# A seven-product down projection for the second group of the gated layer, with block 0's sum held in DRAM, and another written order of the opening

## The chip, the cores and the metric

The kernel runs on one core of a Trainium2 chip. The metric is the device time of one execution in microseconds (us), the median of three runs. The core's engines run side by side and each works through its own queue in the order in which the program writes it: TensorE (PE in the profile, with its weight loads as PEld), VectorE (DVE), ScalarE (ACT), GpSimd (POOL) and the queue that issues most transfers (SP).

## The reference

Three stages follow each other. The first is a retention layer over 2 batches of 8 heads, 768 positions and 64 features per head; its output is reshaped to 1536 tokens of 512 features. Then comes a gated layer of width 1536, then a leaky layer of width 2048:

```python
state = gamma * state + k_t (x) v_t;  y_t = scale * q_t . state      # per batch and head
xn = x / sqrt(mean(x * x) + 1e-6) * rms_g
x  = (silu(xn @ w_gate) * (xn @ w_val)) @ w_out                      # 512 -> 1536 -> 512
h  = x @ w_in
out = maximum(0.01 * h, h) @ w_out2                                  # 512 -> 2048 -> 512
```

All inputs and the output are float32.

## The kernel before

**Retention.** The 1536 positions are 12 chunks of 128, six for each batch. For a chunk `c` the program computes the scores (`sc`), masks them (`ds`), multiplies with the values (`he`), adds what the state of the chunks before gives (`yi`, with queries decayed by `qs`), and updates the state (`kd` decays the keys, `ou` is the outer product, `up` the update). `kd` runs on DVE for the chunks listed in `KD` and as eight small ACT operations for the others. The norm of two chunks at a time goes `sq`, `fa`, `sa` (squares and sums), `to` (total over features, PE), `me` (mean, DVE), `rs` (power -0.5, POOL), `sp` (spread over rows, PE), `xs` (scale), `hi` and `lo` (a rounded high part and the rest).

**Products with split operands.** A float32 operand is kept as a high and a low part, and a product of two operands is three matmuls: high by high, high by low, low by high. Tokens are in three blocks of 512 (`b` = 0, 1, 2). A full product of one 128-wide slice `f` of a layer for one block is 12 matmuls of 128x512.

**Weights.** The weights arrive as 64-bit raw words (512 KB for each slice, tile pool `raws` with 3 buffers, fetched in the queue of SP at L387). Each is converted by two ACT operations (`P`), five DVE operations (`1`, `2`, `3`, `4`, `L`) and one ACT operation (`H`). Converted weights live in 12 slots of the pool `units`, and in 2 more after the retention stage.

**Groups.** The gated layer has 12 slices in groups 0, 1 and 2 of four (kinds `g`, `v` and the down projection `o`); the leaky layer has 16 slices in groups 3 to 6 (kinds `i` and down projection `p`).

**Quads.** For two slices and the blocks 1 and 2 together, `quad` takes seven half products of 6 matmuls in place of eight (42 matmuls in place of 48); it needs two more weight operands made by sums (`sg4` and `sg5` from `g4` and `g5`), each sum key costing six DVE and two ACT operations. Block 0 takes full products (`whole`). The first two slices, `g0`, `g1`, `v0`, `v1`, are plain.

**Down projections.** `down` takes one slice and one block: the hidden block is split (`upper`, an ACT copy at L611, and `lower`, a DVE subtraction at L619) and goes into four PSUM banks in 12 matmuls. After the last slice of a group and block, `evac1` (gated layer) or `evac2` (leaky layer) adds the four banks into an SBUF sum. For the four groups of the leaky layer (the set `seven`, from `SEVEN = 4`) the blocks 1 and 2 of the down projection take the same seven-product scheme: `gather` collects the hidden tiles, `seventh` issues 6 matmuls for each of seven products of a slice pair, `follow` forms the next operand by a DVE subtraction (L704), and the results go from two banks at a time into the sums by DVE (L767). Block 0 of these groups takes plain `down` and is added into the output in DRAM by an accumulating transfer issued from POOL (L800).

**The order.** Everything up to the fourteenth product is written out by hand in `ORDER`: tokens of two letters and a chunk, conversion steps such as `v0:3`, and from `layers` on the products (`Mg01` is the first eight matmuls of slice g0 in block 1, `Ng01` its other four, `C` its evacuation, `Do00` a down projection, `T`, `Th`, `Tl` the sums for the quads). `LOADS` is the order of the first transfers (`q`, `k` a chunk's queries and keys or keys and values of 512 KB; `m` mask, `d` query decays, `s` state decays, `g` norm gains, `i` identity, `w` a raw weight); `load` then adds `q11` and `k11`. After the fourteenth product, `run` places conversions, sums and splits between the products by a small planner with costs (0.6 and 0.34 us for DVE operations, 2.72 us for a product).

Of the kernel before, what the change touches and what calls it, by code (L numbers as in the profile page):

```python
# [16 lines left out]
P = 128  # L17
# [10 lines left out]
HEAD = "dddd0"  # L28
# [34 lines left out]
def chain_kernel(ctx: ExitStack, tc: tile.TileContext, qk_t, kv, w1, w2, mask, qdec, kdec, sdec, rms_g, ident, out):  # L63
# [19 lines left out]
    ps_acc = ctx.enter_context(tc.tile_pool(name="ps_acc", bufs=1, space=bass.MemoryType.PSUM))  # L83
    attn_pools = ctx.enter_context(ExitStack())
# [5 lines left out]

    mask_sb = const.tile([P, 2, NPAIR, CH], F32, name="mask_sb")
# [299 lines left out]
    def open_unit():  # L391
# [12 lines left out]
        if src is None:  # L404
# [229 lines left out]
    def down(gi, f, b):  # L634
        kinds, fs = groups[gi]
        L = kinds[-1]
        key = (L, f, b)
        upper(key)
        lower(key)
        accumulate(L, gi, f, b, f == fs[0], f == fs[-1], L == "o" or b > 0)  # L640
        used(f"{L}{f}")
        if f == fs[-1]:
            banks = acc.pop("b")
            first = gi in (0, len(G1))
            by_copy = first or L == "p" and b == 0 and gi < len(groups) - 1
            later.append(("a" if by_copy else "v", 2.4, lambda: (evac1 if L == "o" else evac2)(gi, b, banks)))
        placed[0] = order.index(key) + 1

    def evac1(gi, b, banks):
        if gi == 0:  # L650
            acc[b] = xp.tile([P, 4, 512], F32, tag=f"acc{b}", name=f"x2acc{b}")
        last = gi == len(G1) - 1
        own = range(2, 4) if b == 2 else range(4)
        if last:
            x2h[b] = xp.tile([P, 4, 512], F32R, tag=f"xh{b}", name=f"x2h{b}")
            x2l[b] = xp.tile([P, 4, 512], F32R, tag=f"xl{b}", name=f"x2l{b}")
        for m in range(4):
            dst = acc[b][:, m, :]
            if gi == 0:
                nc.scalar.activation(out=dst, in_=banks[m], func=AF.Copy)  # L660
            else:
                nc.vector.tensor_tensor(out=dst, in0=banks[m], in1=dst, op=ALU.add)  # L662
        if last:
            def high(m):
                nc.scalar.activation(out=x2h[b][:, m, :], in_=acc[b][:, m, :], func=AF.Copy)

            def low(m):
                nc.vector.tensor_tensor(
                    out=x2l[b][:, m, :], in0=acc[b][:, m, :], in1=x2h[b][:, m, :].bitcast(F32), op=ALU.subtract
                )  # L670

            highs, lows = ([lambda m=m, do=do: do(m) for m in own] for do in (high, low))
            if b == 2:
                one, two = slice(0, 2), slice(2, 4)
                ops = sums_of(
                    acc, x2h, x2l, acc[1][:, one], acc[1][:, two], x2h[2][:, one], x2l[2][:, one], extra()[:, two]
                )
                first_of = [lambda i=i: [ops[n]() for n in (f"{i}", f"h{i}")] for i in range(4)]
                sums.extend(first_of[:2] + [ops["l1"]] + highs + [ops["l0"]] + lows)
                sums.extend([first_of[2], ops["l2"], first_of[3], ops["l3"]])  # L680
            else:
                sums.extend(highs + lows)
# [35 lines left out]

    def seventh(gi, n, f):
        fs = groups[gi][1]  # L720
        key = ("q", f, n)
# [8 lines left out]
        names = f"p{f}", f"p{f + 1}", f"sp{f}", f"sp{f + 1}"  # L730
# [153 lines left out]
    def place(n, key, own=None):  # L884
# [3 lines left out]
        if n == "i" and key[1] == 0:  # L888
            return extra()[:, key[0] % 4, :]
# [46 lines left out]
    def quad(n, f):  # L936
# [62 lines left out]
    def plan():  # L999
# [12 lines left out]
        for gi, (kinds, fs) in enumerate(groups):  # L1012
# [26 lines left out]
            if gi in seven:  # L1039
# [247 lines left out]
```

## Time and profile before

| what | us |
|---|---|
| median of three runs | 582.78 |
| lowest and highest | 582.76, 582.89 |
| the profiled execution | 583.3 |
| its span, first to last instruction | 581.3 |

The profile describes one execution. Its span is 2.0 us shorter than that execution's own time, and that execution is 0.52 us above the median. PE is busy for 98% of the span, DVE for 87%, ACT for 61%.

### The profile page before, as it was taken

Reading aid. Unit: us, or ns where it says so; the run is one execution under the profiler, and the core shown is the slowest. Engines: PE = TensorE matmul, PEld = TensorE weight load, DVE = VectorE, ACT = ScalarE, POOL = GpSimd, SP = SyncE. Lnnn points to the kernel's source line nnn. Section 1 sums busy time; section 2 is a strip of 40 time slices with the busy share of each in tenths; the row PEclk is TensorE's granted clock in tenths of the full one; section 3 lists DMA queues with packets and bytes.
Section 4 is the critical chain, followed back from the end, with each engine's and each line's share of the span. In section 5 each row is a group of like instructions: output and inputs, shape, how many; then the busy total and the mean of one; then the engine's idle time right before and its main releaser. Section 6 shows DMA issues by size and latency. Waiting matters only on the chain.

```text
span 581.3 us, 8448 instructions
## 1 busy us (share of the span) xinstructions
PE 571.3 (98%) x3107; PEld 471.1 (81%) x3107; DVE 505.8 (87%) x921; ACT 355.9 (61%) x652; POOL 26.6 (5%) x28
## 2 busy tenths in 40 slices
PE   7899999999999999999999999999999999999997
PEld 4788788888888888888888878888888888888885
DVE  4899999999578579697688999999999999997793
ACT  2689656776565464554564667877856885676330
POOL 2332100000000000000000000000000020002000
PEclk9999999999999999999999999999999999999999
DMA  8991240433222221221411111113411353111545
GB/s 327 408 392 59 73 144 1 145 110 115 67 73 73 72 74 31 78 72 38 144 37 36 38 36 37 57 53 108 173 39 43 109 142 78 36 37 19 127 85 133
DMA packets 34072, 56.97 MB, mean 98 GB/s; under 512 B 19184, under 2 KB 19312, under 8 KB 34032
## 3 DMA queue, kind: packets, MB, share of 16 engines
q1 hardware_dynamic: 32736, 54.34, 28.9%
q0 software_dynamic: 1152, 2.10, 2.5%
q8 instruction: 24, 0.39, 0.3%
q14 instruction: 16, 0.13, 0.1%
q10 hardware_dynamic: 144, 0.00, 0.0%
HBM read 50.14 MB, written 6.29 MB: 97 GB/s over the span
## 4 chain that ended last, share of the span: by engine, by line
PE 88%; DMA 6%; DVE 3%; ACT 2%; issue 1%; SPq 0%; POOL 0%; DVEq 0%; POOLq 0%; ACTq 0%
PE ao L603 17%; PE iX L931 8%; PE ap L603 7%; PE X L738 7%; PE i L574 7%; PE v L574 7%; PE g L574 6%; PE Z L738 6%; PE vX L931 5%; PE gX L931 5%; PE iZ L931 4%; PE vZ L931 2%; PE gZ L931 2%; DMA qkv<-in_qk_t 2%; PE iY L931 2%; DMA qkv<-in_kv 2%
## 5 line engine op out<-in xcount | busy, mean ns | idle before, releaser
L603 PE MATMUL ap<-w_p,gp_0h 128*128 128x512 f32 x128 | 39.4, 389 | 0.0
L574 PE MATMUL g<-xh,w_g 128*128 128x512 f32 x128 | 31.8, 390 | 0.0
L574 PE MATMUL i<-x2h,w_i 128*128 128x512 f32 x128 | 31.8, 389 | 0.0
L574 PE MATMUL v<-xh,w_v 128*128 128x512 f32 x128 | 31.7, 390 | 0.0
L603 PE MATMUL ao<-go_0h,w_o 128*128 128x512 f32 x96 | 31.5, 389 | 0.0
L603 PE MATMUL ao<-go_2h,w_o 128*128 128x512 f32 x96 | 31.1, 390 | 0.1
L603 PE MATMUL ao<-go_1h,w_o 128*128 128x512 f32 x96 | 30.5, 389 | 0.0
L800 POOL DMA_DIRECT2D out<-more x8 | 7.2, 1078 | 461.7 <-ACT more L796 461.5
L574 PEld LDWEIGHTS g<-xh,w_g 128*128 128x128 f32 x128 | 23.9, 188 | 5.2 <-issue 0.2
L574 PEld LDWEIGHTS i<-x2h,w_i 128*128 128x128 f32 x128 | 24.0, 188 | 5.0
L603 PEld LDWEIGHTS ap<-w_p,gp_0h 128*128 128x128 f32 x128 | 24.0, 188 | 5.0
L574 PEld LDWEIGHTS v<-xh,w_v 128*128 128x128 f32 x128 | 24.0, 188 | 4.9
L603 PE MATMUL ap<-w_p,gp_0l 128*128 128x512 f32 x64 | 24.9, 389 | 0.0
L879 DVE TENSOR_TENSOR g<-v,g 128x512 f32<-128x512 f32 x16 | 10.9, 688 | 14.5 <-PE v L574 14.5
L869 ACT ACTIVATE more<-i 128x512 f32<-128x512 f32 x16 | 9.5, 594 | 21.5 <-PE i L574 21.5
L603 PEld LDWEIGHTS ao<-go_2h,w_o 128*128 128x128 f32 x96 | 18.0, 188 | 4.2 <-issue 0.5
L603 PEld LDWEIGHTS ao<-go_0h,w_o 128*128 128x128 f32 x96 | 18.0, 188 | 3.7
L603 PEld LDWEIGHTS ao<-go_1h,w_o 128*128 128x128 f32 x96 | 18.0, 188 | 3.7
L931 PE MATMUL iZ<-x2h,w_si 128*128 128x512 f32 x64 | 20.3, 391 | 0.0
L931 PE MATMUL iX<-th,w_si 128*128 128x512 f32 x64 | 19.8, 391 | 0.0
L662 DVE TENSOR_TENSOR x2acc<-ao,x2acc 128x512 f32<-128x512 f32 x24 | 15.5, 686 | 4.1 <-PE ao L603 4.1
L603 PE MATMUL ao<-go_2l,w_o 128*128 128x512 f32 x48 | 18.7, 389 | 0.0
(294 smaller groups left out, 1730.8 us busy)
## 6 DMA issues: line engine op xcount, KB each, us to landing
raw_i<-in_w SPq DMA_DIRECT2D x16, 512.0 KB, 3.7
raw_p<-in_w SPq DMA_DIRECT2D x16, 512.0 KB, 3.7
raw_g<-in_w SPq DMA_DIRECT2D x12, 512.0 KB, 3.6
raw_v<-in_w SPq DMA_DIRECT2D x12, 512.0 KB, 3.6
raw_o<-in_w SPq DMA_DIRECT2D x12, 512.0 KB, 4.1
qkT<-in_qk_t SPq DMA_DIRECT2D x7, 512.0 KB, 6.9
kv<-in_kv SPq DMA_DIRECT2D x7, 512.0 KB, 8.1
qkv<-in_qk_t SPq DMA_DIRECT2D x5, 512.0 KB, 10.6
```

Source lines behind the costliest of these rows:

```text
L574: nc.tensor.matmul(out=dst, lhsT=lhs, rhs=rhs, start=(n == 0), stop=(n == len(pairs) - 1), skip_group_check=True)
L603: nc.tensor.matmul(out=acc["b"][m], lhsT=lhs, rhs=rhs, start=(start and n == 0), stop=(stop and n == 2))
L662: nc.vector.tensor_tensor(out=dst, in0=banks[m], in1=dst, op=ALU.add)
L738: nc.tensor.matmul(out=acc[side][m], lhsT=lhs, rhs=rhs, start=(start and f == fs[0] and k == 0), stop=(f == fs[-2] and k == 2), skip_group ...
L800: nc.gpsimd.dma_start(out=rows, in_=dst, accum_op=ALU.add)
L869: nc.scalar.activation(out=a, in_=x, func=AF.Prelu, alpha=0.01)
L879: nc.vector.tensor_tensor(out=a, in0=x, in1=a, op=ALU.mult)
L931: nc.tensor.matmul(out=dst, lhsT=lhs, rhs=rhs, start=(start and n == 0), stop=(n == 5), skip_group_check=True)
```

## The change

It has two parts.

**Group 1 joins `seven`.** `SEVEN1 = (1,)` puts the second group of the gated layer into the set. Its down projection for the blocks 1 and 2 becomes seven half products for each slice pair. Its `o` weights get sums (`so4`, `so6`), and come after all its `g` and `v` weights in the queue. Its hidden tiles of block 0, and three temporary tiles, go into the tile `extra()`, which until then held block 0's sum of the gated layer. That sum is now kept in DRAM (`held`): after group 0 four ACT copies and four stores from SP; after group 1 four ACT copies, four accumulating stores from POOL and four loads from SP; after group 2 four DVE additions.

**Another opening.** `LOADS` and `ORDER` are replaced. The same operations stand in `ORDER` up to the fourteenth product but for these: `kd2` moves from DVE to ACT; `sg2:h`, `sg2:l`, the five steps of `sv2` that stood there, `o2:P` and `o3:P` are left to the planner, and `Th3` and `Tl3` come in from it. Among the loads, `d` and `q1` now come ahead of `s`, `g` and `q3` come later, `q7` comes one place earlier, and `k9` is last but for chunk 11.

```diff
-HEAD = "dddd0"
 OVER = 1.5
 COST = {n: ("a", 1.2) if n == "P" else ("a", 0.54) if n == "H" else ("v", 0.34 if n in "12" else 0.6) for n in "P1234HL"}
 COST_SUM = {n: ("a", 0.54) if n in "Hh" else ("v", 0.34 if n in "1234" else 0.6) for n in "123H4hLl"}
 TWICE = "gvi"
 SEVEN = 4
+SEVEN1 = (1,)
+HEAD = "dddd0"
 RAWS = 3
 WARM = 7
-LOADS = "q0 k0 m g s k1 q1 d q2 q3 k2 k3 q4 k4 q5 w w q6 w q7 k6 k8 k7 k5 i q8 q9 k9 q10 k10"
+LOADS = "q0 k0 m d q1 s k1 q2 k2 k3 g q3 k4 q4 q5 w w q6 q7 w k6 i k8 k7 k5 q8 q9 q10 k10 k9"
 EARLY = 5
 FIXED = 14
 PLAIN = ("g0", "g1", "v0", "v1")
@@ -41,21 +42,20 @@
 BLOCKS = [512, 512, 512]
 
 
-KD = (0, 1, 2, 3, 6, 7)
+KD = (0, 1, 3, 6, 7)
 ORDER = """
-sc0 kd0 ou0 ds0 tb ts wm1 tk he0 load kd1 up0 sc1 sq0 qs1 xg0 ou1 ds1 qs2 sc2 up1 fa0 yi1 qs3 ds2 he1 kd2 sa0 ou2 kd3
-sq1 sc3 xg1 fa1 up2 qs4 yi2 ds3 kd4 ou3 sa1 sc4 up3 qs5 sc5 ds4 g0:P yi3 ds5 ou4 g1:P g0:1 he2 up4 g0:2 he3 g1:1 sq2
...
-he7 v0:H xs0 kd10 he6 me1 sa5 g1:3 sc10 v0:L sq6 g1:4 sq7 ou9 fa6 xg6 sc11 rs1 up9 ds10 xg7 yi8 ds11 g1:H yi9 hi0 qs11
-ou10 o0:P he8 lo0 to2 up10 sq8 he9 fa7 xg8 sa7 sa6 me2 g1:L to3 sq9 sp1 fa8 rs2 me3 xg9 yi10 xs1 rs3 v1:P yi11 fa9
...
-Mv11 sv2:1 sg2:H sg2:3 Cv01 sg2:L Nv11 sv2:2 sg2:4 sv2:H sv2:3 Mv02 T2 sg2:h Cv11 Th2 Nv02 sg2:l Tl2 o3:P Mv12 sv2:4
-o2:P T3 Nv12 Cv12 Cv02
+wm1 sc0 kd0 ou0 ds0 he0 load qs1 ts tb sq0 up0 sc1 tk kd1 ds1 qs2 ou1 yi1 up1 kd2 fa0 sa0 sc2 kd3 xg0 he1 ds2 qs3 ou2
...
+sa2 g0:L ou7 xg4 fa4 he5 sa3 up7 sa4 ou8 v0:2 sq5 g1:3 he6 xg5 v0:3 sp0 fa5 v0:4 sq6 sc8 xs0 qs9 xg6 sc9 v0:H ds8 qs8
+yi7 kd10 ds9 to1 qs10 he7 me1 up8 kd9 fa6 sc11 sa5 sa6 g1:4 yi8 ds11 rs1 sq7 xg7 sc10 qs11 g1:H to2 ds10 ou9 v1:P sp1
...
+Cg02 v2:L Th1 g3:2 T2 g3:3 Mg12 Th2 Tl1 Tl2 Ng12 Mv01 g3:4 Cg12 T3 g3:H v3:P g3:L Nv01 sg2:1 Th3 Mv11 v3:1 sg2:2 v3:2
+sg2:H Tl3 Nv11 sg2:L Mv02 Cv11 v3:3 Cv01 Nv02 v3:4 Mv12 sg2:3 v3:H Cv02 v3:L sg2:4 Nv12 Cv12
...
+    dram = ctx.enter_context(tc.tile_pool(name="dram", bufs=1, space=bass.MemoryType.DRAM))
+    held = [dram.tile([P, 512], F32, name=f"held{i}") for i in range(4)]
...
-    seven = set(range(len(groups) - SEVEN, len(groups)))
+    seven = set(range(len(groups) - SEVEN, len(groups))) | set(SEVEN1)
+
+    def of_seven(n, f):
+        return any(n == groups[gi][0][-1] and f in groups[gi][1] for gi in seven)
+
 
     def doubled(n, f):
-        if n == "p":
-            return any(f in groups[gi][1] for gi in seven)
+        if n in "op":
+            return of_seven(n, f)
         return n in TWICE and f"{n}{f}" not in PLAIN
 
     wq = []
     for gi, (kinds, fs) in enumerate(groups):
         pairs_of = [(n, f) for f in fs[::2] for n in kinds]
         if gi in seven:
-            pairs_of.sort(key=lambda t: kinds.index(t[0]))
+            pairs_of.sort(key=lambda t: t[0] == kinds[-1])
...
-            if n == "p":
+            if n in "op":
...
-            by_copy = first or L == "p" and b == 0 and gi < len(groups) - 1
+            by_copy = gi in (0, len(G1)) or b == 0 and gi not in (len(G1) - 1, len(groups) - 1)
...
+        if b:
+            if gi == 0:
+                acc[b] = xp.tile([P, 4, 512], F32, tag=f"acc{b}", name=f"x2acc{b}")
+            for m in range(4):
+                dst = acc[b][:, m, :]
+                if gi == 0:
+                    nc.scalar.activation(out=dst, in_=banks[m], func=AF.Copy)
+                else:
+                    nc.vector.tensor_tensor(out=dst, in0=banks[m], in1=dst, op=ALU.add)
+            if not last:
+                return
...
+        acc[0] = extra()
+        for m in range(4):
+            t = acc[0][:, m, :]
+            if last:
+                nc.vector.tensor_tensor(out=t, in0=banks[m], in1=t, op=ALU.add)
+                continue
+            nc.scalar.activation(out=t, in_=banks[m], func=AF.Copy)
+            if gi == 0:
+                nc.sync.dma_start(out=held[m], in_=t)
+            else:
+                nc.gpsimd.dma_start(out=held[m], in_=t, accum_op=ALU.add)
+                nc.sync.dma_start(out=t, in_=held[m])
         if last:
+            high, low = x2_parts(0)
+            sums.extend([lambda m=m, do=do: do(m) for do in (high, low) for m in range(4)])
+
...
+        L = groups[gi][0][-1]
+        q = AS[L]
...
+            t = {(k, b): made.pop((L, f + k, b)) for k in range(2) for b in (1, 2)}
+            made[q, f, 1], made[q, f, 3], made[q, f, 2] = t[0, 1], t[1, 2], t[1, 1]
+            turns[q, f] = t
+
+    AS = {"o": "r", "p": "q"}
...
+        total = y2 if L == "p" else acc
...
-        if n == "i" and key[1] == 0:
+        if key[1] == 0 and (n == "i" or of_seven("o", key[0])):
...
-                q[m] = scratch(f"{n}{m}_{f}")
+                if n == "v" and f % 4 == 2 and of_seven("o", f):
+                    q[m] = extra()[:, 3 if m == "u2" else 2, :]
+                else:
+                    q[m] = scratch(f"{n}{m}_{f}")
...
+            if gi in seven and L == "o":
+                wholes = [lambda n=n, f=f: put((f"{n}{f}",), lambda: whole(n, f, 0, xh, xl)) for f in fs for n in kinds[:-1]]
+                for f in fs[::2]:
+                    for n in kinds[:-1]:
+                        own = [(fill or wholes).pop(0) for _ in range(2)]
+                        for i7, (keys, step) in enumerate(quad(n, f)):
+                            put(keys, step)
+                            if i7 in BEHIND[2] and own:
+                                own.pop(0)()
+            elif gi in seven:
...
+                        order.append((AS[L], f, n))
+                        keys = (f"{L}{f}", f"{L}{f + 1}", f"s{L}{f}", f"s{L}{f + 1}")[SIDES[n][0]], "half"
```

## Rows read from the trace of the kernel before

**Rows 1.** Windows by stage: us, then busy us and count of each engine
```profile
0.00:53.82 53.82, 47.96 (x775) 39.67 (x775) 43.83 (x90) 35.39 (x102) 17.30 (x18) 1.00 0.80 310
53.82:95.39 41.57, 41.31 (x211) 33.48 (x210) 40.93 (x68) 28.09 (x49) 2.07 (x2) 1.00 0.31 89
95.39:141.63 46.24, 46.24 (x206) 38.30 (x205) 45.04 (x85) 32.11 (x58) 0.00 (x0) 1.00 0.33 99
141.63:234.11 92.48, 92.48 (x410) 76.60 (x409) 69.16 (x126) 50.38 (x87) 0.00 (x0) 1.00 0.25 72
...
444.27:474.19 29.92, 29.92 (x133) 24.77 (x133) 29.68 (x60) 22.66 (x41) 0.00 (x0) 1.00 0.33 105
```

**Rows 2.** Chain that ended last, in order of time: start, us, what
```profile
27.66 9.15 DMA qkv<-in_kv
...
69.74 3.89 PE g L574 x16
...
121.23 1.36 PE vX L931 x6
...
225.95 8.16 PE ao L603 x36
...
326.59 0.13 issue
...
566.67 10.89 PE ap L603 x48
```

**Rows 3.** Timeline: operations that began as a transfer landed
```profile
20.08 2.02 ACT L163 ACTIVATE kd<-kv,kdecs 128x64 f32<-128x64 f32 x8 [2.41 <-DMA kv<-in_kv]
...
21.41 1.16 PE L182 MATMUL sc<-qkv 64*128 64x128 f32 x16 [0.81 <-DMA qkv<-in_qk_t]
...
30.23 2.02 ACT L163 ACTIVATE kd<-qkv,kdecs 128x64 f32<-128x64 f32 x8 [0.82 <-DMA qkv<-in_kv]
...
36.89 2.12 ACT L163 ACTIVATE kd<-qkv,kdecs 128x64 f32<-128x64 f32 x8 [1.11 <-DMA qkv<-in_kv]
```

**Rows 4.** Timeline of DVE after the fourteenth product
```profile
99.51 0.42 DVE L459 TENSOR_SCALAR wa_o<-wa_o 128x512 f32<-128x512 f32 x1
99.84 0.69 DVE L425 TENSOR_TENSOR w_sv<-wa_v,w_sv 128x512 fp32r<-128x512 f32 x1
100.44 0.42 DVE L463 TENSOR_SCALAR wa_o<-wa_o 128x512 int32<-128x512 int32 x1
100.78 0.69 DVE L425 TENSOR_TENSOR w_sv<-wa_v,w_sv 128x512 fp32r<-128x512 f32 x1
```

**Rows 5.** Operations of a seven-product group, 408 to 467.9 us: busy us, mean ns
```profile
L767 DVE TENSOR_TENSOR y2acc<-X,y2acc 128x512 f32<-128x512 f32 x8 | 5.2, 682 | 0.0
...
L418 DVE TENSOR_TENSOR wa_p<-wa_p,wa_p 128x256 f32<-128x256 f32 x6 | 2.5, 418 | 0.0
...
L704 DVE TENSOR_TENSOR iu<-is,iu 128x512 f32<-128x512 f32 x2 | 1.4, 686 | 0.0
```

**Rows 6.** Block 0's accumulating stores (L800) and the copies ahead of them
```profile
L800 POOL DMA_DIRECT2D out<-more x8: 856/1092/1308, 474.5 to 536.8; - x8
...
DMA to landing us min/median/max: 4.0/5.7/7.0
...
L796 ACT ACTIVATE more<-ap x12: 590/600/612, 413.7 to 535.9; 128x512 f32<-128x512 f32 x12
```

**Rows 7.** Timeline of PE in the norm steps between products
```profile
65.04 0.66 PE L307 MATMUL norm<-ident_sb,nr 128*64 128x128 f32 x8
...
65.52 0.35 PE L290 MATMUL norm<-ones,ss 128*64 128x1 f32 x8
```

**Rows 8.** Timeline: the opening's first norm product, chunk 1's scores, chunk 9's outer product
```profile
8.44 0.61 PE L1111 MATMUL norm<-sdecs,one_of 128*128 128x4 f32 x4 [1.19 <-DMA sdecs<-in_sdec]
...
12.10 1.23 DVE L194 TENSOR_TENSOR a<-sc,mask_sb 128x1024 f32<-128x1024 f32 x1 [1.02 <-PE sc L182]
...
41.90 0.69 PE L208 MATMUL u<-qkv,kd 128*64 128x64 f32 x16
```

More of the change, by code (lines that the diff above doesn't have):

```diff
@@ L621, in lower @@
             spend("v", 0.6)
-            if key[0] == "q":
-                follow(key[1], key[2])
+            if key[0] in "qr":
+                follow(*key)
                 spend("v", 0.6 if key[2] in (1, 3, 5, 6) else 0.0)
@@ L649, in evac1 @@
     def evac1(gi, b, banks):
-        if gi == 0:
-            acc[b] = xp.tile([P, 4, 512], F32, tag=f"acc{b}", name=f"x2acc{b}")
         last = gi == len(G1) - 1
-        own = range(2, 4) if b == 2 else range(4)
+        if b:
[9 more added lines that the diff above has]
+                return
+            highs, lows = ([lambda m=m, do=do: do(m) for m in range(2 * b - 2, 4)] for do in x2_parts(b))
+            if b == 1:
+                sums.extend(highs + lows)
+                return
+            one, two = slice(0, 2), slice(2, 4)
+            ops = sums_of(acc, x2h, x2l, acc[1][:, one], acc[1][:, two], x2h[2][:, one], x2l[2][:, one], extra()[:, two])
+            both = [lambda i=i: [ops[n]() for n in (f"{i}", f"h{i}")] for i in range(4)]
+            sums.extend(both[:2] + [ops["l1"]] + highs + [ops["l0"]] + lows + [both[2], ops["l2"], both[3], ops["l3"]])
+            return
@@ L654, in evac1, with x2_parts @@
         if last:
+            high, low = x2_parts(0)
+            sums.extend([lambda m=m, do=do: do(m) for do in (high, low) for m in range(4)])
+    def x2_parts(b):
+        if b not in x2h:
             x2h[b] = xp.tile([P, 4, 512], F32R, tag=f"xh{b}", name=f"x2h{b}")
             x2l[b] = xp.tile([P, 4, 512], F32R, tag=f"xl{b}", name=f"x2l{b}")
[L657 to L682, printed above, removed]
+        def high(m):
+            nc.scalar.activation(out=x2h[b][:, m, :], in_=acc[b][:, m, :], func=AF.Copy)
@@ L684, in chain_kernel, with low @@
+        def low(m):
+            nc.vector.tensor_tensor(
+                out=x2l[b][:, m, :], in0=acc[b][:, m, :], in1=x2h[b][:, m, :].bitcast(F32), op=ALU.subtract
+            )
+        return high, low
     SIDES = {
@@ L691, in gather, with follow @@
     def gather(gi):
+        L = groups[gi][0][-1]
+        q = AS[L]
         for f in groups[gi][1][::2]:
-            t = {(k, b): made.pop(("p", f + k, b)) for k in range(2) for b in (1, 2)}
-            made["q", f, 1], made["q", f, 3], made["q", f, 2] = t[0, 1], t[1, 2], t[1, 1]
-            turns[f] = t
+            t = {(k, b): made.pop((L, f + k, b)) for k in range(2) for b in (1, 2)}
+            made[q, f, 1], made[q, f, 3], made[q, f, 2] = t[0, 1], t[1, 2], t[1, 1]
+            turns[q, f] = t
+    AS = {"o": "r", "p": "q"}
     turns = {}
     touched = set()
-    def follow(f, n):
-        t = turns[f]
+    def follow(q, f, n):
+        t = turns[q, f]
         def less(out, in0, in1):
@@ L755, in seventh @@
         banks = acc[side]
+        total = y2 if L == "p" else acc
         fresh = gi == len(G1) and (b, row) not in touched
-        touched.add((b, row))
-        if b not in y2:
+        if L == "p":
+            touched.add((b, row))
+        if b not in total:
             y2[b] = xp.tile([P, 4, 512], F32, tag=f"acc{b}", name=f"y2acc{b}")
@@ L762, in put @@
             for m in range(2):
-                dst = y2[b][:, 2 * row + m, :]
+                dst = total[b][:, 2 * row + m, :]
                 if fresh:
@@ L1045, in plan @@
                             own.pop(0)()
-                wholes = [lambda f=f: put((f"i{f}",), lambda: whole("i", f, 0, h, l)) for k, f in enumerate(fs) if not first or str(k) not in HEAD]
+                wholes = [lambda f=f: put((f"i{f}",), lambda: whole("i", f, 0, x2h, x2l)) for k, f in enumerate(fs) if not first or str(k) not in HEAD]
+            if gi in seven:
                 for n, more in zip((1, 5, 6, 3, 7, 2, 4), (1, 0, 1, 0, 1, 0, 1)):
                     for f in fs[::2]:
-                        order.append(("q", f, n))
-                        keys = (f"p{f}", f"p{f + 1}", f"sp{f}", f"sp{f + 1}")[SIDES[n][0]], "half"
+                        order.append((AS[L], f, n))
+                        keys = (f"{L}{f}", f"{L}{f + 1}", f"s{L}{f}", f"s{L}{f + 1}")[SIDES[n][0]], "half"
                         put(keys, lambda n=n, f=f, gi=gi: seventh(gi, n, f))
```

28 lines of the change are left out of this document (14 added, 14 removed).

## The prediction

> **What bounds the kernel now.** I read the windows by stage first [rows 1]. In the stage up to the first product of the gated layer (53.82 us) no engine is busy throughout: PE 47.96, DVE 43.83, ACT 35.39, and the transfers run at 310 GB/s on average. From there on PE is busy nearly all the time. The chain of waits says the same with other words [rows 2]: until 36.8 us it runs through transfers of queries and keys, then through ACT and DVE, and from 69.74 us to 577.56 it is PE without a break but for 0.13 us at 326.59. In that part time is a count of matmuls: 36 take 8.16 us, so one takes 0.2267 and twelve take 2.72. A matmul that is left out there is won, as long as DVE and ACT still deliver operands in time. How near DVE is to its limit differs by stage [rows 1]: 45.04 of 46.24 us while group 0 ends, 69.16 of 92.48 in group 1, and 29.68 of 29.92 in half a group of the leaky layer, where it is full and PE still never waits.
>
> The opening is paced by arrivals up to about 37 us. Operations that began as their transfer landed [rows 3] lie on a line: `kd4` at 20.08 us, the scores of chunk 5 at 21.41, `kd8` at 30.23, `kd9` at 36.89. In LOADS there are 8 pieces of 512 KB between `k4` and `k8`: 10.15 us, so 1.27 for one piece; `k9`, five pieces on, needs 6.6 us, so 1.3.
>
> **The change part by part: group 1.** Counted on PE: the down projections of blocks 1 and 2 took 4 slices x 2 blocks x 12 = 96 matmuls; the seven products take 2 pairs x 7 x 6 = 84. Twelve fewer, at 0.2267 each: 2.72 us less. The group falls from 408 matmuls (92.48 us, which is its window [rows 1]) to 396 (89.76 us).
>
> What it adds on DVE, by the distance from one start to the next when nothing lies between [rows 4]: 0.60 us for a tensor operation of 512 columns, 0.34 for a short one. That a bank addition and a subtraction in SBUF cost the same, and that a sum of 256 columns costs the short price, is seen in a group that has the scheme already (682 and 686 ns, against 418) [rows 5]. Six more low parts (14 for 8), eight subtractions of `follow`, two more bank additions (14 for blocks 1 and 2 where there were 12 for three blocks), and four low parts of `so4` and `so6`: 20 x 0.60 = 12.0. Their eight sums: 8 x 0.34 = 2.7. Together 14.7 us, so DVE's 69.16 become 83.9 of 89.76: 93%. This is hidden by the 23 us that DVE idles in this group now; were that cover gone, 14.7 us would show. ACT gets 6 high parts, 4 for the sums and 4 copies of block 0's banks, about 0.6 each [rows 6]: 8.4 on 50.38 of 92.48 [rows 1], hidden. I cost both at nothing.
>
> Block 0's sum through DRAM: four stores after group 0 and four round trips after group 1. The loads back stand in SP's queue behind the accumulating stores, and the next raw weights stand behind them. One such store occupies POOL for 1.09 us and lands 4.0 to 7.0 us after issue [rows 6], so SP is held at most 4 x 1.09 + 7.0 = 11.4 us. A group has 12 raw weights in 92.48 us, one for each 7.7 us; with one of three raw tiles waiting, the other two give 15.4 us of conversions. Hidden, with 4 us to spare. The loaded sum is wanted only when group 2 ends, some 70 us on.
>
> [...]
>
> **The opening.** The operations up to the fourteenth product are nearly the same. DVE loses `kd2` (0.60), `sg2:l` (0.60) and four sums of `sv2` (1.36), and gets `Tl3` (1024 columns, so about twice 0.60): 1.4 less. PE's order from `layers` on is unchanged but for small norm steps. What was put off must come later: `sv2` is first read at 121.23 us [rows 2], where its low parts are ready at 101.4 now [rows 4]; 20 us of slack. `sg2` is read by the third product of the first quad, 5.4 us after the fourteenth product, and needs one ACT and one DVE operation, 1.2 us, behind two gate products: enough.
>
> How much time PE can win here: between 53.82 and 95.39 us 14 x 12 matmuls take 38.08 of 41.57 us; three spreads (0.66) and two totals (0.35) [rows 7] take 2.7; 0.8 is waiting. With 1.4 us less on DVE, which is busy for 40.93 of these 41.57 us [rows 1], 2.2 is the most I can find. How much it can lose: `s` now stands behind `d` and `q1`, 768 KB, so 1.9 us; its first use was at 8.44 us and would be at 10.3 [rows 8], which delays the key decays and the masked scores of chunk 1 (12.10 now) by about 0.9, since DVE waited 1.02 there. But `q5`, for which PE waits at 21.41 [rows 3], keeps its place, so this delay is swallowed by then. `k9` comes two pieces later: 36.8 + 2.6 = 39.4, and with 2.0 us of ACT [rows 3] at 41.4, where the outer product of chunk 9 ran at 41.90 [rows 8]. In the new PE order it stands behind the scores of 11 and 10, the state product of 8 and a total, and comes some 2.5 us later; but the program has fewer steps behind it. So the bounds are 2.2 won and 2.5 lost. I take 0.4 won, near the middle: arrivals and work are nearly equal, DVE's queue is a little shorter.
>
> **The sum.** The profiled execution took 583.3: 583.3 - 2.72 - 0.4 = 580.2. The median lies 0.52 below that execution: 579.7.
>
> **The rivals.**
> - *The opening gains more* (1 to 2.2): for it speaks that PE waits and DVE idles there; against it that arrivals pace the first 37 us. 577.9 to 579.1.
> - *The opening loses 1 to 2.5*, through `s` or `k9`: 581.1 to 582.6. Against it: both delays meet a wait that is there already.
> - *DVE becomes the bound as group 1 ends* (the other side). While the 84 matmuls and 4 whole products run, 29.9 us, DVE has 14 low parts, 8 subtractions, 14 bank additions and 2 gate products, 38 x 0.60 = 22.8, and the next group's `g8`, `g9`, `sg8`: 4.96 + 2.56 = 7.5. That is 30.3. The leaky layer's groups have the same less the gates, 29.1, and PE doesn't wait there [rows 1]. If `so6` (2.6) slips into this stretch, PE waits 2.9 us and the gain is gone; if a weight (2.5) slips as well, 5.4: 583.3 - 2.72 - 0.4 + 5.4 - 0.52 = 585.1. From 3.9 us of lateness on it is slower by the measure below. Against it: 23 us of idle DVE in the group before.
> - *SP held too long*: past 15.4 us, each further us is one of conversions; at 20 us of holding 4.6 come back, 584.3. [...] That the saving does not show at all, because PE was not the bound, is excluded by the chain but for a part in 50: 582.4.
>
> **How the numbers follow.** Less than 0.2% (1.17 us) can't be told from no change. Forecast (the 12 matmuls, the opening within 1 us of even) 0.60, opening better 0.14, opening worse 0.12, DVE late 0.09, SP 0.03, no saving 0.02. Faster (below 581.6): 0.60 + 0.14 + half of the third, 0.80. Same: the other half, a third of DVE late and the last, 0.11. Slower: the rest, 0.09. The range goes from 577.8, the bound of the gain, to 582.3; the forecast's own is 578.7 to 580.7.
>
> **What would show it.** Group 1 should take 89.8 us from the first matmul of its first quad to that of group 2's, with no piece in the chain but PE, and DVE busy for 84 of them. A wait of PE for a weight or an operand near the start of group 2 is the DVE rival; a fetch at L387 that waits long for a store of `held` is the SP rival. First product at 53 to 54 us, fourteenth ended at 94.5 to 95.5: the opening as forecast. Earlier or later by over 1 us, and the opening's rivals hold. The prediction is wrong if the chain shows DVE or a transfer between 100 and 330 us for more than 1 us.

## The result, and the profile after

The changed kernel takes 590.69 us (median of six executions, 586.79 to 592.95), the kernel before 582.88 (582.76 to 583.15): a ratio of 1.0127 with a 95% interval of 1.0107 to 1.0146. It is 1.3% slower, where 579.7 was forecast. Its times also lie 6 us apart, where those of before lie within 0.4, and they go with the mean granted clock: 586.79 at 0.996, 589.38 at 0.993, 592.95 at 0.988. The profiled execution took 592.0 (span 590.0, clock 0.99).

The windows by stage of the changed kernel, cut at the same events as [rows 1] (first product, end of the fourteenth, and the first quads of groups 1 and 2), then the stage of group 2 up to the gated layer's last four down projections, and three short stretches. Columns: us; busy us and count of PE, PEld, DVE, ACT, POOL; granted clock; DMA share; GB/s.

```profile
0.00:59.87 59.87, 50.74 (x784) 42.97 (x784) 48.59 (x90) 37.49 (x112) 16.12 (x18) 0.94 0.75 287
59.87:101.59 41.72, 41.47 (x205) 33.05 (x202) 40.80 (x66) 26.17 (x44) 6.67 (x3) 1.00 0.26 77
101.59:147.83 46.24, 46.24 (x206) 38.30 (x205) 44.45 (x86) 33.00 (x58) 0.00 (x0) 1.00 0.41 126
147.83:237.59 89.76, 89.76 (x398) 74.36 (x397) 74.34 (x136) 50.55 (x87) 0.00 (x0) 1.00 0.15 47
237.59:334.64 97.05, 94.22 (x409) 77.27 (x408) 80.16 (x151) 55.75 (x97) 4.00 (x4) 0.98 0.37 106
...
15.00:18.00 3.00, 3.00 (x26) 2.67 (x28) 2.88 (x5) 1.33 (x6) 1.26 (x1) 0.51 1.05 418
39.00:41.00 2.00, 2.00 (x25) 2.00 (x24) 1.90 (x4) 0.00 (x0) 0.00 (x0) 0.50 1.05 391
...
274.00:277.00 3.00, 2.71 (x6) 2.15 (x7) 2.77 (x6) 2.40 (x5) 0.00 (x0) 0.50 0.17 63
```

Against [rows 1] the stages say where the time is. The stage up to the first product grew from 53.82 to 59.87, +6.05. Up to the fourteenth, +0.15. Group 0 is the same 46.24. Group 1 fell from 92.48 to 89.76, -2.72, with PE busy throughout: the forecast saving is there to the hundredth. Group 2 has PE idle for 2.83 us, and the clock is not 1.00. In three stretches, two in the opening and one in group 2, the granted clock is 0.50 or 0.51; in the stages of before it was 1.00 [rows 1].

The waits of PE in the changed kernel (line <- releaser: us in all, times, longest):

```profile
PE u L210 <- DVE kd L157: 3.6, 2, 2.9
PE vX L961 <- ACT vu L978: 2.7, 1, 2.7
PE u L210 <- ACT xg L271: 2.2, 1, 2.2
PE norm L292 <- DVE xg L326: 1.3, 2, 1.0
```

The first and the third are the opening, the second is group 2. Each of the three long ones stands just ahead of one of the slow stretches. So two places are to be explained.

**The opening.** Timeline of the changed kernel around the first wait, and around the second (start, us, engine and line, idle time before and its releaser):

```profile
9.51 1.26 POOL L173 TENSOR_TENSOR qs<-qkT,qdec_sb 128x512 f32<-128x512 f32 x1 [9.06 <-DMA qkT<-in_qk_t]
9.57 1.61 DVE L1174 TENSOR_TENSOR sdecs<-sdecs 128x4 f32<-128x4 f32 x3 [1.42 <-DMA sdecs<-in_sdec]
11.66 1.83 DVE L1165 TENSOR_TENSOR kdecs<-kdecs,turn 128x8 f32<-128x8 f32 x4
12.01 1.26 POOL L173 TENSOR_TENSOR qs<-qkT,qdec_sb 128x512 f32<-128x512 f32 x1 [1.24 <-DMA qkT<-in_qk_t]
13.41 0.68 DVE L157 TENSOR_TENSOR kd<-kv,kdecs 128x512 f32<-128x512 f32 x1
14.01 1.22 DVE L196 TENSOR_TENSOR a<-sc,mask_sb 128x1024 f32<-128x1024 f32 x1
14.15 0.82 PE L210 MATMUL u<-kv,kd 128*64 128x64 f32 x16 [2.86 <-DVE kd L157]
...
18.55 1.22 DVE L196 TENSOR_TENSOR a<-sc,mask_sb 128x1024 f32<-128x1024 f32 x1 [0.64 <-PE sc L184]
18.60 1.28 POOL L173 TENSOR_TENSOR qs<-qkT,qdec_sb 128x512 f32<-128x512 f32 x1 [1.44 <-PE sc L184]
...
35.06 2.68 POOL L173 TENSOR_TENSOR qs<-qkv,qdec_sb 128x512 f32<-128x512 f32 x2 [3.62 <-DMA qkv<-in_qk_t]
35.12 1.50 DVE L278 TENSOR_TENSOR sq<-sq 128x256 f32<-128x256 f32 x1
36.54 1.35 DVE L283 TENSOR_TENSOR ss<-sq 128x128 f32<-128x128 f32 x1
37.81 0.41 DVE L227 TENSOR_TENSOR state<-u,sdecs 128x256 f32<-128x256 f32 x1
38.33 1.06 PE L210 MATMUL u<-qkv,kd 128*64 128x64 f32 x16 [2.20 <-ACT xg L271]
```

The same DVE operations in the kernel before, its first `qs`, and a later meeting of `ss` with a `qs`:

```profile
8.66 0.55 DVE L1131 TENSOR_TENSOR sdecs<-sdecs 128x4 f32<-128x4 f32 x3
...
9.36 0.78 DVE L1122 TENSOR_TENSOR kdecs<-kdecs,turn 128x8 f32<-128x8 f32 x4
10.05 0.68 DVE L155 TENSOR_TENSOR kd<-kv,kdecs 128x512 f32<-128x512 f32 x1
...
11.51 3.92 POOL L171 TENSOR_TENSOR qs<-qkT,qdec_sb 128x512 f32<-128x512 f32 x3 [11.06 <-DMA qdec_sb<-in_qdec]
...
18.88 1.27 POOL L171 TENSOR_TENSOR qs<-qkT,qdec_sb 128x512 f32<-128x512 f32 x1 [3.44 <-DMA qkT<-in_qk_t]
19.06 1.24 DVE L281 TENSOR_TENSOR ss<-sq 128x128 f32<-128x128 f32 x1
```

The decay table starts 0.91 us later (9.57 for 8.66), which is about the delay that was forecast. But `kd1` starts 3.36 later. Between them three tiny operations took 1.61 us for 0.55 and four others 1.83 for 0.78, and at both times POOL ran a `qs`; that this is the cause is shown further down, by e8_qs_dve. The copy of chunk 0's state, which the new `ORDER` puts ahead of the key decays, adds 0.33.

The meeting has two sides, for `qs` moved as well. In the kernel before it began at 11.51, released by the landing of `d`; now `d` and `q1` come ahead of `s`, and it began at 9.51, 2.0 us earlier. Before, the key decays were done at 10.14 (9.36 + 0.78). Later by 0.91 and by the 0.33 of the copy they would have been done at 11.38, still ahead of 11.51. So the late `s` alone would not have brought the two together; this is worked out from the rows, and no run leaves `s` late with `d` and `q1` late as well.

In the second place `sq` and `ss` took 1.50 and 1.35 us beside two `qs` (0.41 and 0.28 alone, in the same trace), and the state update of chunk 7 and its successor waited behind them. The profile names ACT's `xg` as what released PE there; that was done at 37.79, the update at 38.22, and PE went on at 38.33, so I take it to have waited for the update. The masked scores at 18.55, which read `sc` from PSUM, took 1.22 beside a `qs`, as they did at 14.01, when POOL stood idle.

**Group 2.** Timeline of the changed kernel, of POOL, the queue of SP, ACT and PE:

```profile
257.10 4.00 POOL L687 DMA_DIRECT2D held<-more  x4 [183.51 <-ACT more L683]
263.07 3.41 SPq L688 DMA_DIRECT2D more<-held  x3
266.58 0.37 SPq L393 DMA_DIRECT2D raw_i<-in_w  x1
...
272.05 0.66 ACT L537 ACTIVATE wb_i<-raw_i 128x512 int32<-128x512 uint32 x1 [7.47 <-DMA raw_i<-in_w]
272.61 0.62 ACT L486 ACTIVATE w_v<-wa_v 128x512 fp32r<-128x512 f32 x1
273.65 0.58 ACT L978 ACTIVATE vu<-vX 128x512 f32<-128x512 f32 x1
274.29 1.22 PE L961 MATMUL vX<-th,w_sv 128*128 128x512 f32 x2 [2.69 <-ACT vu L978]
```

The four accumulating stores begin at 257.10; SP stands with the loads of `held` behind them, and the next raw weight is fetched only at 266.58. ACT stood 7.47 us before that weight, with a conversion, a high part and the copy of a product bank `vu` behind it in its queue. PE needed that bank and stood 2.69 us. The chain of the changed kernel runs through it:

```profile
257.10 0.98 POOL held L687
258.63 7.46 DMA held<-more
...
266.58 5.39 DMA raw_i<-in_w
...
274.29 2.93 PE vX L961 x6
277.21 1.52 PE vZ L961 x6
...
345.81 2.72 PE i L580 x12
```

Six matmuls took 2.93 us where [rows 2] has 1.36 for six of the same kind, and the next six 1.52: 1.57 and 0.16 us more, at a granted clock of 0.50 from 274 to 277 us and 0.94 from 277 to 280. With the wait that is 2.69 + 1.57 + 0.16 = 4.42.

**The account.** The span grew by 8.7 us (590.0 - 581.3). The fourteenth product ended at 101.59 for 95.39: +6.20. From there to the first product of the leaky layer 244.22 us for 242.50: +1.72, that is -2.72 + 4.42 within 0.02. The leaky layer took the same (239.66 for 239.67). After the last matmul 4.53 for 3.74: +0.79, which I cannot account for. 6.20 + 1.72 + 0.79 = 8.71.

### The profile page after: what moved, and what is told of

Read it like the earlier page. It is cut to its first block, busy times and chain, and to the rows that moved or that the text cites. A ratio compares the mean times of both kernels' runs of the same rounds, so it can differ in the third digit from the quotient of the medians.

```text
span 590.0 us, 8517 instructions
## 1 busy us (share of the span) xinstructions
PE 573.2 (97%) x3095; PEld 472.8 (80%) x3095; DVE 521.8 (88%) x948; ACT 362.9 (62%) x674; POOL 33.8 (6%) x32
## 4 chain that ended last, share of the span: by engine, by line
PE 62%; issue 22%; DVE 8%; DMA 4%; ACT 2%; SPq 0%; POOL 0%; ACTq 0%; POOLq 0%; DVEq 0%
PE iX L961 7%; PE ap L609 7%; PE i L580 7%; PE X L766 7%; PE ao L609 6%; PE Z L766 6%; PE iZ L961 4%; PE v L580 3%; PE g L580 3%; PE iY L961 2%; PE vX L961 2%; DMA held<-more 2%; PE gX L961 1%; PE sc L184 1%; DMA sdecs<-in_sdec 1%
## 5 line engine op out<-in xcount | busy, mean ns | idle before, releaser
L609 PE MATMUL ao<-go_2h,w_o 128*128 128x512 f32 x64 | 20.6, 391 | 0.1
L609 PE MATMUL ao<-go_1h,w_o 128*128 128x512 f32 x64 | 20.4, 389 | 0.0
L537 ACT ACTIVATE wb_i<-raw_i 128x512 int32<-128x512 uint32 x16 | 10.7, 671 | 15.3 <-DMA raw_i<-in_w 8.1
L609 PE MATMUL ao<-go_0l,w_o 128*128 128x512 f32 x48 | 18.7, 389 | 0.0
L263 ACT ACTIVATE sq<-y 128x512 f32<-128x512 f32 x12 | 7.2, 603 | 17.8 <-PE y L251 17.8
L580 PE MATMUL v<-xl,w_v 128*128 128x512 f32 x64 | 17.4, 393 | 0.0
L580 PE MATMUL g<-xl,w_g 128*128 128x512 f32 x64 | 17.2, 391 | 0.0
```

The costliest lines, as they stand in the source:

```text
L263: nc.scalar.activation(out=s["sq"], in_=s["y"], func=AF.Square)
L537: nc.scalar.activation(out=m, in_=low.bitcast(U32), func=AF.Copy, scale=2.0 ** -29)
L580: nc.tensor.matmul(out=dst, lhsT=lhs, rhs=rhs, start=(n == 0), stop=(n == len(pairs) - 1), skip_group_check=True)
L609: nc.tensor.matmul(out=acc["b"][m], lhsT=lhs, rhs=rhs, start=(start and n == 0), stop=(stop and n == 2))
```

## The experiments

Theory A: two causes that have nothing to do with each other, the opening (some 6 us) and the hold of SP's queue at `held` (some 4 us), and behind both a saving of 2.7. The rivals are that one of them is a consequence of the other, that the seven-product scheme itself is late, and, within the opening, that arrivals rather than POOL's neighbourhood or the clock make the loss. All ten runs at a glance (the kernel before measured 582.90 to 582.97 beside them). The last two columns come from the one profiled execution of each run: when the fourteenth product ended, and how long the span goes on after the last matmul. The kernel before has 95.39 and 3.7 there, the changed kernel 101.59 and 4.5.

| run | us | range | ratio to before, 95% | fourteenth product ended | after the last matmul |
|---|---|---|---|---|---|
| e1_opening | 590.21 | 586.56 to 590.73 | 1.0110 (1.0080 to 1.0141) | 103.05 | 3.8 |
| e2_group | 585.18 | 583.58 to 586.64 | 1.0038 (1.0026 to 1.0050) | 95.08 | 3.8 |
| e3_group_pool | 580.93 | 580.80 to 581.15 | 0.9964 (0.9950 to 0.9978) | 95.42 | 4.4 |
| e4_after_pool | 585.64 | 585.41 to 587.13 | 1.0051 (1.0036 to 1.0066) | 98.79 | 5.2 |
| e5_s_early | 582.65 | 582.43 to 582.76 | 0.9994 (0.9985 to 1.0003) | 96.12 | 5.3 |
| e6_up7 | 586.17 | 584.29 to 587.66 | 1.0057 (1.0039 to 1.0074) | 99.62 | 5.3 |
| e7_both | 583.69 | 582.75 to 584.12 | 1.0012 (1.0002 to 1.0021) | 97.25 | 5.3 |
| e8_qs_dve | 582.86 | 581.68 to 583.25 | 0.9994 (0.9984 to 1.0003) | 97.11 | 4.0 |
| e9_warm | 583.27 | 582.56 to 586.23 | 1.0008 (0.9997 to 1.0019) | 96.64 | 5.2 |
| e10_early_dve | 581.72 | 581.47 to 582.57 | 0.9982 (0.9972 to 0.9991) | 96.04 | 4.5 |

**e1_opening: the opening alone.** The kernel before with the new `LOADS`, `KD` and `ORDER`, and nothing of group 1.

```diff
-LOADS = "q0 k0 m g s k1 q1 d q2 q3 ...
+LOADS = "q0 k0 m d q1 s k1 q2 k2 ...
-KD = (0, 1, 2, 3, 6, 7)
+KD = (0, 1, 3, 6, 7)
...
```

> The kernel before with the new opening alone (LOADS, KD and ORDER), group 1 as it was. Theory A, the opening loses by itself: the fourteenth product ends some 6 us later, as in the changed kernel (101.6 for 95.4 us), and the time is about 589. Theory B, the opening is even as forecast and what comes late there comes from the seven-product group: about 582.5.

Measured 590.21: the opening loses 7.2 us by itself, with the same two waits of PE:

```profile
PE u L207 <- DVE kd L154: 3.5, 2, 2.8
...
PE u L207 <- ACT xg L268: 2.2, 1, 2.2
```

Behind the first of them the granted clock is lower for longer than in the changed kernel: 0.69 from 12 to 15 us and 0.50 from 15 to 18 in this profile, where the changed kernel has 0.92 and 0.51.

**e2_group: group 1 alone.** The changed kernel with `LOADS`, `KD` and `ORDER` of before.

> The changed kernel with the opening of before, so the seven-product group 1 and the sum in DRAM alone. Theory A, the loads of the held sum keep SP from fetching and ACT stands in front of a raw weight: 2.72 us won, 2.7 to 4.4 lost to one wait of PE in the first pair of group 2, so 583 to 584.5, and ACT waits some 7 us for a raw weight. Theory B, the group's own work on DVE is the limit: several waits of PE for DVE, 585 or more. As forecast, without a wait: 580.1.

Measured 585.18, 0.7 above the band of theory A; by the number alone it would be theory B. The trace decides for A: there is no wait of PE for DVE in group 2. PE has one new wait there, 2.1 us for `vu`, ACT stood 7.45 us before `raw_i`, and behind that the clock fell. The windows of e2_group there:

```profile
270.00:272.00 2.00, 2.00 (x6) 1.52 (x6) 2.00 (x4) 1.42 (x3) 0.00 (x0) 0.51 0.00 0
```

So neither cause brings the other. The opening costs 7.2, the hold 4.25 (e3_group_pool, below); less the saving of 2.0 that e3 shows, 9.4 would be left, and 7.8 was measured. The ranges of e1 and of the changed kernel, 4 and 6 us wide, cover the difference, and e1's longer stretch of low clock is a part of it; I don't split it further.

**e3_group_pool: the loads of `held` out of SP's queue.** e2_group, with them issued from POOL, where they wait behind the stores and nothing else does.

```diff
-                nc.sync.dma_start(out=t, in_=held[m])
+                nc.gpsimd.dma_start(out=t, in_=held[m])
```

> As the run before, but the four loads of the held sum are issued by POOL, behind its own accumulating stores, so that SP goes on fetching. Theory A, SP's queue was the wait: it is gone, and the 2.72 us show in full, 580.1. Theory B, the group's DVE or ACT work was the wait: no better than the run before.

Measured 580.93, 0.4% faster than before, and 4.25 us below e2_group. The queue of SP, first in e2_group, then in e3_group_pool:

```profile
256.02 3.22 SPq L689 DMA_DIRECT2D more<-held  x3
259.35 0.42 SPq L394 DMA_DIRECT2D raw_i<-in_w  x1
```

```profile
254.75 19.08 SPq L394 DMA_DIRECT2D raw_i<-in_w  x4
```

The fetch begins 4.6 us earlier. After 54 us no wait of PE is left among its longest, and the windows of e3_group_pool over groups 0 to 2 show it busy throughout, at a clock of 1.00:

```profile
95.39:141.63 46.24, 46.24 (x206) 38.29 (x205) 45.13 (x85) 32.69 (x58) 0.00 (x0) 1.00 0.41 123
141.63:231.39 89.76, 89.76 (x398) 74.32 (x397) 73.83 (x136) 49.96 (x87) 0.00 (x0) 1.00 0.17 49
231.39:323.95 92.56, 92.51 (x409) 76.27 (x407) 79.93 (x151) 55.56 (x97) 6.45 (x8) 1.00 0.37 111
```

The first product of the leaky layer starts at 335.19 for 337.89: 2.70 us won. Of these 2.04 reach the median (580.93 - 582.97); the tail after the last matmul is again 0.7 longer (4.44 for 3.74; in e2_group it was 3.8). This kernel beats both that were compared.

**e4_after_pool: the changed kernel with the same edit.**

> The changed kernel with the four loads of the held sum issued by POOL. Theory A: only the wait in group 2 goes, 4.4 us with the clock that falls behind it, so about 586 in place of 590.7. Theory B, the wait has another cause: no change.

Measured 585.64, 5.05 below the changed kernel: the wait of group 2 is gone (4.4), and in this profile the second wait of the opening as well, since `sq` began 0.3 us ahead of POOL's `qs` and was done in its usual time. What is left against e3_group_pool is 4.71, and the two programs differ in the opening alone. In their profiles 3.37 of it lie ahead of the end of the fourteenth product (98.79 for 95.42) and 0.8 behind the last matmul (5.2 for 4.4); why the end is longer, no run shows. The following runs start from e4.

**e5_s_early: `s` back to the front.**

```diff
-LOADS = "q0 k0 m d q1 s k1 q2 ...
+LOADS = "q0 k0 m s d q1 k1 q2 ...
```

> The changed kernel with POOL's loads of the held sum (585.6, fourteenth product ended at 98.8 us), and in LOADS the state decays s ahead of d and q1 again, as before. Theory A, the late s sets the first wait: the tables of decays are built some 1.5 us earlier, before POOL's qs1 starts, PE waits under 1 us for kd1 in place of 2.3 and keeps its clock, and 1 to 2 us of it reach the end: about 584. Theory B, as I forecast, chunk 5's queries swallow that delay: 585.6, no change.

Measured 582.65, 3.0 below e4, more than expected; the ten executions lie within 0.3 us. PE waited 1.2 us for `kd1`, a little more than the 1 us expected. The three operations on the state decays take 0.55 again, and the key decays have POOL beside them for a part (timeline of e5_s_early):

```profile
10.04 1.34 DVE L1165 TENSOR_TENSOR kdecs<-kdecs,turn 128x8 f32<-128x8 f32 x4
```

The fourteenth product ended at 96.12 for 98.79 in e4. So the late `s` was not swallowed by the later arrivals. The edit moves only the tables: POOL's `qs` begins at 9.48, for 9.53 in e4.

**e6_up7: the update of chunk 7 ahead of `sq` and `ss`.**

```diff
-... ou7 xg4 fa4 he5 sa3 up7 sa4 ou8 ...
+... ou7 up7 xg4 fa4 he5 sa3 sa4 ou8 ...
```

> The same kernel of 585.6 us with the state update of chunk 7 moved ahead of the first sums of chunk 4 and the second of chunk 3 in DVE's order. Theory A, those two sums stand still beside POOL's two decays of queries near 35 us in some executions, and PE then waits for the update: such executions (the changed kernel's profile, 101.6 us at the fourteenth product) are gone, all runs near the best, 585.4, and no spread beyond 0.5. Theory B, the spread of the changed kernel has another cause (the clock, or landings): the spread stays at 2 us or more.

Measured 586.17 (584.29 to 587.66), no better than e4: the expectation failed. In its profile the second wait is not there, the first one (2.9 us) is, and the times still spread over 3.4 us. So the second wait is not needed for the spread.

**e7_both: e5 and e6 together.**

> Both edits, s early and the update of chunk 7 moved ahead. Theory A: the sum of the two, about 584 without spread. If the rest of the loss in the opening lies in the order of chunks 8 to 11 (k9 last), it stays over 582.5 all the same; if not, it comes to the 580.9 of the run with the opening of before.

Measured 583.69, near the 584 that was expected, but not as the sum of two gains: it is 1.0 us worse than e5 alone, and the executions lie 1.4 apart. In its profile `sq` falls at 35.78 and took 1.50, its length beside POOL's `qs` in the changed kernel, and the totals of the norm waited 3.0 us (1.3 in e5). By that length a delay mended in one place moved the meeting to another.

**e8_qs_dve: no POOL beside the tables.** e6, with `qs` of chunks 1 and 2 on DVE, behind `kd1` and `kd2`. `s` stays late.

```diff
-            nc.gpsimd.tensor_tensor(out=s["qs"], ...
+            (nc.vector if c in (1, 2) else nc.gpsimd).tensor_tensor(out=s["qs"], ...
-... he0 load qs1 ts tb sq0 up0 sc1 tk kd1 ds1 qs2 ou1 yi1 up1 kd2 fa0 ...
+... he0 load ts tb sq0 up0 sc1 tk kd1 qs1 ds1 ou1 yi1 up1 kd2 qs2 fa0 ...
```

> The kernel with the update of chunk 7 moved ahead and s late, with qs1 and qs2 done by DVE (0.6 us each) behind the key decays of chunk 1, so that POOL stands idle while DVE builds the tables. Theory A, two operations in SBUF of DVE and one of POOL exclude each other: the table of state decays takes 0.55 us and not 1.6, the table of key decays 0.8 and not 1.8, and PE waits about 1 us less for kd1, though DVE has 1.2 us more to do. Theory B, these operations are slow for another cause (transfers, the clock): they still take 1.6 and 1.8.

Measured 582.86, 3.3 below e6; in the profiles 2.51 of it are there when the fourteenth product ends (97.11 for 99.62), and 1.3 lie behind the last matmul (4.0 for 5.3), which this edit doesn't explain. The same operations of DVE in e8_qs_dve, as late as in the changed kernel, but alone:

```profile
9.49 0.56 DVE L1174 TENSOR_TENSOR sdecs<-sdecs 128x4 f32<-128x4 f32 x3 [0.71 <-DMA sdecs<-in_sdec]
10.74 0.77 DVE L1165 TENSOR_TENSOR kdecs<-kdecs,turn 128x8 f32<-128x8 f32 x4
```

0.56 and 0.77, the times of before. PE waits 0.6 us for `kd` where it waited 2.9. So it is POOL's operation beside them that stretches them, not their place in time or the transfers.

**e9_warm: the clock by itself.** e4 with eleven matmuls without use behind the scores of chunk 1, to keep PE busy while it waits for `kd1`. They are extra work.

```diff
-... sq0 up0 sc1 tk kd1 ds1 ...
+... sq0 up0 sc1 wm2 tk kd1 ds1 ...
-"wm": lambda c: keep_warm(c, 4)
+"wm": lambda c: keep_warm(c, 11 if c == 2 else 4)
```

> The kernel of 585.6 us (new opening, loads of the held sum by POOL, s late) with eleven more warm-up matmuls of PE behind the scores of chunk 1, where PE waits 2.3 us for kd1. Nothing is won for the wait itself. [...] Theory B, the wait alone counts and the clock loss is swallowed by the transfers: 585.6, spread as before.

Measured 583.27, 2.4 below e4, where I had looked for about 1, and not the 585.6 of theory B. I had looked for all executions within 0.5 as well: nine of ten lie between 582.56 and 583.52, the tenth, 586.23, does not, so that was missed. The window in which the changed kernel had 0.51, and the key decays, in e9_warm:

```profile
15.00:18.00 3.00, 3.00 (x56) 2.71 (x54) 2.79 (x6) 1.36 (x6) 0.56 (x1) 1.00 1.02 408
```

```profile
11.62 1.89 DVE L1165 TENSOR_TENSOR kdecs<-kdecs,turn 128x8 f32<-128x8 f32 x4
```

The tables are as slow as ever, yet PE runs at 1.00 and does 56 matmuls in these 3 us instead of 26 (34 in e4, at a clock of 0.60). The fourteenth product ended at 96.64 for 98.79, with the same 5.2 us after the last matmul: 2.15 of the 3.37 us by which e4's opening is behind that of e3 are what the wait does to the clock after it. What makes the spread is not settled by it: three of e4's four executions lie within 0.31 and one is 1.4 above them.

A lower clock need not cost time: in the profile of e3_group_pool it was 0.52 from 9 to 12 us, and the fourteenth product ended at 95.42, 0.03 from the kernel before.

**e10_early_dve: e5 with `qs` of chunks 1 and 2 on DVE.**

> The kernel with s early (582.65 us; fourteenth product ended at 96.1), with qs1 and qs2 done by DVE behind kd1. Theory A, what is left of the opening's loss is DVE standing still beside POOL (the table of key decays still took 1.34 us there, for 0.77): 0.5 us better, 582.1, and the table takes 0.8. Theory B, the rest lies later, with chunks 8 to 11: 582.6 or, with 1.2 us more DVE work, worse.

Measured 581.72, 0.9 below e5 and 0.2% faster than before; the key decays took 0.78. But the fourteenth product ended at 96.04 for 96.12, only 0.08 earlier; the rest of the gain lies behind the last matmul (4.5 us for 5.3). So the number meets theory A, and its mechanism, half a microsecond from DVE in the opening, is not shown. The run stays 0.79 above e3_group_pool, with the fourteenth product at 96.04 for 95.42. No run here says whether this last part is `k9`, the norm or another meeting of DVE and POOL.

## Why the prediction was wrong

**The saving: right.** Twelve matmuls fewer at 0.2267 were to give 2.72. Group 1 took 89.76 us as forecast, the changed kernel and e3_group_pool alike, and e3 won 2.70 up to the leaky layer. "Hidden on DVE and ACT" was right as well. DVE was busy for 74 us of the group and not 84: of the 14.7 that I had counted 5.2 are seen there (69.16 to 74.34), and the stage of group 2 grew by 6.9 (from 73.22 in the kernel before to 80.16), so a part was probably placed later. The rival of a late DVE fell, since PE never waits in group 1 and, in e3, is busy for 92.51 of 92.56 us in group 2. Two of its sums were off, without weight for the result: a slipped `so6` makes 3.0 us and not 2.9 (30.3 + 2.6 - 29.9), and with the 0.4 won in the sum it takes 4.3 us of lateness, not 3.9, to be clearly slower.

**The step that failed most: "this delay is swallowed by then", in the opening.** I let the late `s` delay the tables by about 0.9 us, and they did start 0.91 later. The error is what I let follow from it: that the wait for `q5` at 21.41 would take it up, with a loss of 2.5 at the worst and 0.4 won as the value. Measured is +6.20. Two links were missing. The first is what DVE loses beside POOL: the same edit of `LOADS` that made the tables 0.91 later let POOL's `qs` begin 2.0 earlier, the seven small operations met it, and the delay of `kd1` became 3.36 (0.91, 1.06, 0.33 for the copy, and 1.05; e8: alone the operations take 0.56 and 0.77). The prediction counted what `d` and `q1` cost `s`, and not what they release sooner. The trace of before had the sign, shown above: an `ss` that took 1.24 us at 19.06 beside a `qs` that ran from 18.88 to 20.15, and I did not ask what the moved operations would stand beside. The second is the clock: after 2.86 us of idle PE it worked at 0.51 through the next stretch (e9: 2.4 us, with the tables still slow). The second wait and its stretch of 0.50 repeat this at 36 us. The shares overlap, since the loss beside POOL makes the wait behind which the clock falls; they are not to be added. The bound of 2.5 was too narrow because it knew only work and arrivals, not what a wait costs afterwards.

What stood beside a `qs` fared differently by its inputs: the state decays, with both in SBUF, took 1.61 us for 0.55; the masked scores, which read `sc` from PSUM, took 1.22 with a `qs` beside them and without. Whether PSUM makes the difference no run sets apart.

**The second step that failed: "Hidden, with 4 us to spare", for SP's hold.** Its length was right: 11.4 us at most were forecast, and from the first store at 257.10 to the fetch at 266.58 it was 9.5. The cover was wrong. I counted 15.4 us of conversions from two raw tiles in hand; but ACT took its steps in order here (the conversion at 272.05, the high part at 272.61, the copy of `vu` at 273.65), and its queue had already reached the first step of the missing weight. From then on the cover is what PE can do without ACT, and that was 4.8 us of the 7.47 (7.47 - 2.69). The rival "SP held too long", put at 3 in 100 and begun only "past 15.4 us", is what happened, after 9.5 us of holding. Its price of 4.6 was for 20 us of holding, so that 4.25 was measured (e2 to e3) is luck. The stores were not the miss: the four occupied POOL for 4.00 us together, and each measured 1.05 to 1.75 us and landed after 5.9 to 8.3, for 0.86 to 1.31 and 4.0 to 7.0 in [rows 6]; that is slower, and the hold still stayed within the 11.4 us.

**The chances.** The loss through `s` had its rival, with the right load and too low a ceiling. None of them had both misses at once, and none the clock.

**Left open.** The time after the last matmul, which is 3.7 to 3.8 us in the kernel before, e1 and e2 and 4.0 to 5.3 in the others, and goes into every median; the last 0.62 of the opening in e10 (96.04 for 95.42); why e6 spreads over 3.4 us and e4 over 1.7.

## What to carry to other kernels

When an operation moves in time, ask what runs beside it at its new place, and what else the same edit lets start earlier: the small operations of DVE with both inputs in SBUF took 1.61 us for 0.55 beside one of POOL here, so put such pairs apart, or put there what lost nothing in this case (the masked scores from PSUM, 1.22 us either way). A wait of PE can cost nearly as much again through the clock: the one of 2.3 us in e4 cost 2.15 more, the one of 2.69 in group 2 cost 1.73 (1.57 + 0.16), and matmuls without use in the wait prevented it in e9. And a transfer that waits for another belongs in a queue in which nothing urgent stands behind it (4.25 us from e2 to e3); count the cover of a late fetch from the first instruction that needs it, on any engine that takes its steps in order, as ACT did here.

## What the runs showed of the hardware

- Seven operations of 4 and 8 columns took 3.44 us beside POOL (1.61 + 1.83) and 1.33 alone (0.55 + 0.78); the two groups lost 1.06 and 1.05 us, near the 1.26 of the one POOL operation beside each, and more than their own time.
- The granted clock fell to 0.50 or 0.51 after PE had stood 2.86, 2.20 and 2.69 us (windows from 15, 39 and 274 us of the changed kernel). In e9 eleven matmuls in the wait kept it at 1.00. PE works visibly on at the lower level: 26 matmuls for 56 in the same 3 us.
- The kernels with such a wait in the opening (the changed kernel, e1, e4, e6) have times that spread over 1.7 to 6.2 us. Without it e5 spreads over 0.3, but e7 and e8 over 1.4 and 1.6, and e9 over 3.7 by one execution. So the wait goes with the spread, and is not shown to be all of it.
